# Summary scores on the whole array, and a planner that picks PSUM banks by first release, with measured durations and later landings

## The chip, the cores and the metric

The kernel runs on one core of one Trainium2 chip. The metric is the time on the device in microseconds (us), the median over runs. Lines such as L939 are lines of the kernel before.

The engines have these names in the profile: PE is TensorE (matrix products, written to the eight banks of PSUM), PEld its loading of weights, DVE is VectorE, ACT is ScalarE, POOL is GpSimd, SP is SyncE, which here only issues DMAs. Each engine works through a queue of its own in order; semaphores hold an instruction until its inputs are there.

## The reference, cut to what matters

Attention in which each query sees its neighbours within 16 positions and one summary per block of 32 keys, then eight experts over all tokens, weighted by a routing matrix that is normalised by rows and columns eight times. There are 4 batches, 8 heads, 768 positions and 64 values per head; block is 32 and window 16; N is 3072 tokens of 512 values, E is 8 and F 1024.

```python
    k_sum = k.reshape(B, H, nb, block, D).max(axis=3)
    v_sum = v.reshape(B, H, nb, block, D).mean(axis=3)
    scores_l = scale * np.matmul(q, k.transpose(0, 1, 3, 2))
...
    mask_l = np.abs(pos[:, None] - pos[None, :]) < window
    scores_s = scale * np.einsum('bhsd,bhnd->bhsn', q, k_sum)
    scores_s = scores_s + np.log(block)
    scores_l_m = np.where(mask_l, scores_l, -1000000000.0)
...
    a = a / (np.sum(a, axis=-1, keepdims=True) + 1e-09)
    v_all = np.concatenate([v, v_sum], axis=2)
    return np.matmul(a, v_all).astype(np.float32)
...
    P = np.exp(logits)
    for _ in range(8):
        P /= P.sum(1, keepdims=True) + 1e-09
        P /= P.sum(0, keepdims=True) + 1e-09
        P *= N / E
...
    for e in range(E):
        h = np.maximum(x @ w1[e], 0.0)
        ye = h @ w2[e]
        out += P[:, e:e + 1] * ye
```

## The kernel before

**Stages.** The first part (up to about 169 us) holds the attention, expert 0, the routing and the beginning of expert 1, interleaved. The rest (L1217 on) runs experts 1 to 7 in a fixed order written out by hand, with a scheme that forms a block product from seven instead of eight smaller products; the change does not touch its instructions.

**Attention.** The unit of work is a pair of heads; there are 16 pairs, four for each of the four batches. Pairs 0 to 3 are worked in two halves of 384 queries (`pair_half`, L691), so that expert 0 can begin early; pairs 4 to 15 are worked whole (`pair_whole`, L721). For each pair, POOL issues the loads of k, q and v (`load_pair`, L642); k and q are transposed, on PE and copied out by ACT or DVE (`tr`, L306, and `tr_out`), or for pairs 12 to 15 by a DMA from SP (`tr_dma`, L318). The local scores (`scores`, L379) are matmuls of 64 rows, one head in each half of the array; ACT takes the exponential, DVE multiplies with the band mask (`masks`), and for whole pairs DVE copies the strips that reach into the next block of 128 keys into a shared tile (`edges`). `key_max` (L336) reduces the keys of the pair to 24 maxima for each of the two heads in one DVE instruction, with the head in the upper or lower 64 partitions of `ksT`. The summary scores multiply these with the queries: `summaries` (L427) for a half pair, two matmuls of 64 rows by 32 columns; `summaries2` (L436) for a whole pair, four of them, into two banks. `block_sums` (L351) forms the block sums of v with constant weights `m_blk`, six different ones of 128 columns. `values` and `values_h` bring it together in a bank `av`; DVE normalizes (`normalize`, L510); the result is transposed on PE (`to_xT`) or, for pairs 10 to 14, by a DMA from SP (`x_dma`, L323), and lands in `xT`. `near_values` (L369) is four small DMAs from SP for each whole pair.

**Expert 0 and routing.** As soon as a batch's `xT` is there, `expert0` (L758) computes it in halves of 384 tokens: eight hidden units (L208), relu on ACT or DVE, then six projections of half the depth (L218). `logits` (L537) gives the routing scores of a batch, with `gate` (L794) as its entry in the plan. After the last batch, `bridge` (L1120) adds the eight row and column normalisations, in turn on DVE (sums, reciprocals), POOL (multiplication) and PE (column totals), and the first four groups of expert 1.

**The planner.** All of this is written as units with an engine, a cost in us, dependencies, a priority and the PSUM buffers that they open and use (`Plan.add`). `Plan.order` (L58) simulates the engines when the kernel is built, and emits the units in the order of simulated start times; that becomes each engine's queue. Nothing of it is decided on the chip: if an input comes later than the plan thought, the engine waits and everything behind it in that queue waits too. Four things set the simulated times: the cost of a unit; `HOP`, 0.15 us between engines; `RESHAPE`, 0.1 us when PE goes from one form of the array (`shape`) to another; and `lag`, the time from the end of an issue until a DMA has landed. Gaps of PE of over 0.22 us before the first hidden unit is evacuated are filled with idle matmuls (`keep_busy`, L562, and L852).

**PSUM banks.** The stage has tags m (3 banks), a (3 banks) and s (one buffer of two banks). Within a tag the banks are used in turn: a unit that opens a buffer takes the bank that follows the last one, and waits until that bank's last reader is done. The pools give the tiles out in the same turn (`bank`, L258).

**Loads.** The loads form one chain on POOL (`load`, L637): each is issued after the one before. In the plan a load lands 0.4 us after its share of the DMA engines' time.

## Time and profile before

| | us |
|---|---|
| median of the runs shown (3) | 676.51 |
| their range | 675.13 to 679.61 |
| the profiled execution | 676.52 |
| its span, from the first to the last instruction | 674.8 |
| PE busy in the span | 660.7 |
| DVE busy | 578.9 |
| ACT busy | 404.6 |
| POOL busy | 132.6 |
| mean granted clock of PE | 0.999 |

The profile is a page with several parts and a trace that answers questions. A line of a group reads: line of the kernel, engine, operation, output<-inputs by the program's names, shapes, count, then the busy time in us and the mean of one in ns, then the idle time of the engine just before them and what ended it. A timeline line reads: start, length, engine, line, operation; several that follow each other are merged, with their count. Lists of waits read: who waited, for whom, us in total, how often, the longest. Matmuls are pipelined, so the recorded length of one is longer than the time until the next one starts; the pace is read from start to start.

### The profile page before, as it was taken

Reading aid. Unit: us, or ns where it says so; the run is one execution under the profiler, and the core shown is the slowest. Engines: PE = TensorE matmul, PEld = TensorE weight load, DVE = VectorE, ACT = ScalarE, POOL = GpSimd, SP = SyncE. Lnnn points to the kernel's source line nnn. Section 1 sums busy time; section 2 is a strip of 40 time slices with the busy share of each in tenths; the row PEclk is TensorE's granted clock in tenths of the full one; section 3 lists DMA queues with packets and bytes.
Section 4 is the critical chain, followed back from the end, with each engine's and each line's share of the span. In section 5 each row is a group of like instructions: output and inputs, shape, how many; then the busy total and the mean of one; then the engine's idle time right before and its main releaser. Section 6 shows DMA issues by size and latency. Waiting matters only on the chain.

```text
span 674.8 us, 13527 instructions
## 1 busy us (share of the span) xinstructions
PE 660.7 (98%) x5107; PEld 434.0 (64%) x5107; DVE 578.9 (86%) x1434; ACT 404.6 (60%) x787; POOL 132.6 (20%) x177
## 2 busy tenths in 40 slices
PE   8899998999999999999999999999999999999996
PEld 4566655555666666666666666666666666666665
DVE  7778896776799988998799988998899879998885
ACT  5678885565777765555655565555555565556551
POOL 8599631121101010201010010101020101100001
PEclk9999999999999999999999999999999999999999
DMA  9999999000513050311422051306031232201224
GB/s 119 187 145 146 135 117 154 1 1 1 79 11 37 1 79 1 36 13 23 57 23 27 1 78 11 39 1 79 1 34 16 25 55 23 26 1 53 88 80 157
DMA packets 124018, 36.46 MB, mean 54 GB/s; under 512 B 110384, under 2 KB 121136, under 8 KB 123952
## 3 DMA queue, kind: packets, MB, share of 16 engines
q0 software_dynamic: 104672, 26.22, 43.4%
q1 hardware_dynamic: 18464, 8.83, 6.7%
q8 instruction: 40, 0.66, 0.4%
q10 hardware_dynamic: 816, 0.54, 0.2%
q14 instruction: 26, 0.21, 0.1%
HBM read 52.45 MB, written 6.29 MB: 87 GB/s over the span
## 4 chain that ended last, share of the span: by engine, by line
PE 88%; DMA 5%; DVE 4%; POOL 1%; issue 1%; ACT 0%; DVEq 0%; ACTq 0%
PE xy L939 36%; PE pg L933 16%; PE pb L933 11%; PE pa L933 10%; PE yps L218 5%; PE hps L208 4%; DMA xT<-xs 2%; DMA qst<-in_q_dram 2%; DMA w<-in_moe_w_dram 1%; PE sg L344 1%; PE tkq L315 1%; DVE xs L521 1%; PE vs L354 1%; PE tx L528 0%; DVE hf L883 0%
## 5 line engine op out<-in xcount | busy, mean ns | idle before, releaser
L939 PEld LDWEIGHTS <-hf 128*128 128x128 f16 x2352 | 230.1, 98 | 96.9 <-issue 2.3
L939 PE MATMUL xy<-w,hf 128*128 128x256 f16 x1312 | 183.4, 273 | 0.1
L939 PE MATMUL xy<-ws,hf 128*128 128x256 f16 x984 | 147.6, 273 | 0.4
L199 ACT ACTIVATE hf<-pg 128x512 f16<-128x512 f32 x84 | 50.2, 597 | 150.4 <-PE pg L933 150.4
L1075 DVE SCALAR_TENSOR_TENSOR out_acc<-xy,P_sb,out_acc 128x512 f32<-128x512 f32 x164 | 115.0, 742 | 1.7 <-PE xy L939 1.7
L880 DVE TENSOR_TENSOR hf<-hf 128x512 f16<-128x512 f16 x252 | 99.8, 423 | 8.8
L933 PE MATMUL pa<-xT,w 128*128 128x512 f16 x336 | 99.9, 379 | 0.0
L933 PEld LDWEIGHTS <-w 128*128 128x128 f16 x672 | 65.8, 98 | 43.8 <-issue 0.2
L883 DVE TENSOR_TENSOR hf<-pb,c 128x512 f16<-128x512 f32 x84 | 58.1, 691 | 38.8 <-PE pb L933 35.0
L184 POOL DMA_DIRECT2D w<-in_moe_w_dram x56 | 41.7, 756 | 221.1 <-PE pg L933 192.4
L933 PEld LDWEIGHTS <-ws 128*128 128x128 f16 x504 | 49.3, 98 | 25.3
L967 ACT COPY c<-pg 128x512 f32<-128x512 f32 x84 | 49.3, 586 | 22.4 <-PE pg L933 22.4
L883 DVE TENSOR_TENSOR hf<-pg,c 128x512 f16<-128x512 f32 x84 | 57.1, 679 | 0.7 <-PE pg L933 0.7
L952 ACT COPY pg<-pa 128x512 f32<-128x512 f32 x84 | 47.9, 570 | 4.8
L199 ACT ACTIVATE hf<-pa 128x512 f16<-128x512 f32 x84 | 50.6, 602 | 0.0
L960 ACT COPY c<-pb 128x512 f32<-128x512 f32 x84 | 49.7, 592 | 0.7 <-PE pb L933 0.5
L933 PE MATMUL pg<-xTs,w 128*128 128x512 f16 x168 | 50.0, 379 | 0.1
L933 PE MATMUL pg<-xTs,ws 128*128 128x512 f16 x168 | 50.0, 379 | 0.0
L933 PE MATMUL pb<-xT,ws 128*128 128x512 f16 x168 | 50.0, 379 | 0.0
L933 PE MATMUL pg<-xT,w 128*128 128x512 f16 x168 | 50.0, 379 | 0.0
L933 PE MATMUL pb<-xTs,ws 128*128 128x512 f16 x168 | 50.0, 379 | 0.0
L208 PE MATMUL hps<-xT,w 128*128 128x384 f16 x256 | 48.9, 326 | 0.0
(143 smaller groups left out, 819.6 us busy)
## 6 DMA issues: line engine op xcount, KB each, us to landing
w<-in_moe_w_dram POOLq DMA_DIRECT2D x8, 1024.0 KB, 9.0
w<-in_moe_w_dram POOLq DMA_DIRECT2D x56, 128.0 KB, 3.6
out_dram<-out_acc SPq DMA_DIRECT2D x20, 256.0 KB, 2.0
qst<-in_q_dram POOLq DMA_DIRECT2D x32, 96.0 KB, 6.0
vx<-in_v_dram POOLq DMA_DIRECT2D x16, 192.0 KB, 6.6
kst<-in_k_dram POOLq DMA_DIRECT2D x24, 96.0 KB, 6.2
w<-in_moe_w_dram POOLq DMA_DIRECT2D x2, 512.0 KB, 8.7
kst<-in_k_dram POOLq DMA_DIRECT2D x4, 192.0 KB, 4.9
```

The source lines that it names most:

```text
L184: nc.gpsimd.dma_start(out=t[:, :, h, :], in_=moe_w1[e].rearrange("(dk p) f -> p dk f", p=128)[:, :, f:f + 128])
L199: nc.scalar.activation(out=out, in_=in_, func=AF.Relu, bias=0.0, scale=1.0)
L208: nc.tensor.matmul(hp[:, 0:n], lhsT=w1s[e][:, dk, 128 * f:128 * (f + 1)], rhs=xT[:, dk, t0:t0 + n], start=(dk == 0), stop=(dk == KD - 1))
L218: nc.tensor.matmul(yp[:], lhsT=h[:, f, c * 128:(c + 1) * 128], rhs=w2s[e][:, f, :], start=(f == 0), stop=(f == KF - 1))
L880: nc.vector.tensor_tensor(out=out, in0=in0, in1=in1, op=ALU.subtract)
L883: nc.vector.tensor_tensor(out=out, in0=in0, in1=in1, op=ALU.add)
L933: nc.tensor.matmul(bank[:], lhsT=w[:, dk, :], rhs=x[:, dk, :], start=start and dk == 0, stop=dk == KH - 1, skip_group_check=True)
L939: nc.tensor.matmul(bank, lhsT=a(f)[:, 128 * c:128 * (c + 1)], rhs=w[:, f, :], start=start and f == 0, stop=f == FH - 1, skip_group_check=True)
L952: nc.scalar.copy(out=B["g"][:], in_=B["a"][:])
L960: nc.scalar.copy(out=B["c5"][:], in_=B["b"][:])
L967: nc.scalar.copy(out=B["c2"][:], in_=B["g"][:])
L1075: nc.vector.scalar_tensor_tensor(out=acc, in0=src, scalar=P_sb[:, t, e:e + 1], in1=acc, op0=ALU.mult, op1=ALU.add)
```

## The change

Seven things change, all in the first part.

1. `key_max` writes the maxima to a scratch tile, and a DVE multiply with a constant `own` (ones where the partition belongs to the head, zeros elsewhere) spreads them over a 128-column `ksT`: head 0 in columns 0 to 23 with the lower partitions zero, head 1 in columns 32 to 55 with the upper ones zero, zeros in the rest.
2. The summary scores become one matmul of 128 rows by 128 columns for each half; `summaries2` goes, and whole pairs call `summaries` twice, each with a bank of its own. The exponential reads partitions 0 to 63 in all cases.
3. `m_blk` becomes one strip of 148 columns; the six weights are windows of it that overlap.
4. The planner keeps no turn: a unit takes, of the banks of its tag whose readers are all placed, the one that is released first in the plan. Each bank is a tag of its own in the pool.
5. `HOP` becomes 0.23 us after PE and 0.1 us after any other engine.
6. Costs and lags of units change. The diff shows those that the text speaks of; the costs of the products of expert 0, of `logits` and of the output transposes change by 0.04 us or less, and that of the load of w2 by 0.2.
7. The normalisations' lag for `columns` becomes 0.7 us in place of 2.0 (first) and 1.2.

```diff
-    HOP = 0.15
+    HOP = {"PE": 0.23}
...
     def __init__(self, slots, idle=None):
-        self.slots, self.idle, self.shape = {}, idle, None
-        self.ring, self.turn, self.free, self.waiting = {}, {}, {}, []
+        self.idle, self.shape = idle, None
+        self.ring, self.free, self.waiting, self.now = {}, {}, [], []
...
-            self.slots[t], self.ring[t], self.turn[t] = n, [None] * n, 0
+            self.ring[t] = [None] * n
...
     def order(self):
-        free, ring, turn, waiting = self.free, self.ring, self.turn, self.waiting
+        free, ring, waiting = self.free, self.ring, self.waiting
...
+        def hop(x, e):
+            return 0.0 if x.on == e else self.HOP.get(x.on, 0.1)
+
         def ready(u):
-            t = 0.0
-            for i, b in enumerate(u.opens):
-                old = ring[b.tag][(turn[b.tag] + i) % self.slots[b.tag]]
-                if old is not None:
-                    if any(x.start is None for x in old.users):
-                        return None
-                    t = max([t] + [x.end + (self.HOP if x.on not in u.eng else 0.0) for x in old.users])
+            t, u.slots = 0.0, []
+            for b in u.opens:
+                at = []
+                for n, old in enumerate(ring[b.tag]):
+                    if (b.tag, n) in u.slots or old is not None and any(x.start is None for x in old.users):
+                        continue
+                    at.append((max([0.0] + [x.end + hop(x, "PE") for x in old.users]) if old else 0.0, n))
+                if not at:
+                    return None
+                t0, n = min(at)
+                u.slots.append((b.tag, n))
+                t = max(t, t0)
...
+
+        def take(u):
+            for b, (tag, n) in zip(u.opens, u.slots):
+                ring[tag][n] = b
+            self.now = [n for _, n in u.slots]
...
-                            + [d.end + d.lag + (self.HOP if d.on != e else 0.0) for d in u.deps])
+                            + [d.end + d.lag + hop(d, e) for d in u.deps])
...
-                    ring["m"][turn["m"] % self.slots["m"]] = x.opens[0]
-                    turn["m"] += 1
+                    take(x)
...
+            if u.slots:
+                t0 = max(t, ready(u))
+                t, end = t0, end + t0 - t
...
-            for b in u.opens:
-                ring[b.tag][turn[b.tag] % self.slots[b.tag]] = b
-                turn[b.tag] += 1
...
+            take(u)
...
-        m_blk = attn.tile([128, G, 128], BF16, name="m_blk")
+        m_blk = attn.tile([128, 4 * (G - 1) + 128], BF16, name="m_blk")
...
-        ksT = [attn.tile([128, 32], BF16, name=f"ksT{i}") for i in range(NB)]
+        ksT = [attn.tile([128, 128], BF16, name=f"ksT{i}") for i in range(NB)]
+        own = attn.tile([128, 2, 24], BF16, name="own")
...
         def bank(tag, name, dtype=FP32):
-            pool, n = (mps, 3) if tag == "m" else (aps, NA)
-            return pool.tile([128, 2048 // mybir.dt.size(dtype)], dtype, tag=tag, name=name, bufs=n)
+            n = plan.now.pop(0) if plan.now else 0
+            return (mps if tag == "m" else aps).tile([128, 2048 // mybir.dt.size(dtype)], dtype, tag=f"{tag}{n}",
+                                                     name=name, bufs=1)
...
         def banks2(name, dtype=FP32):
+            plan.now.pop(0)
...
-            nc.vector.tensor_reduce(out=ksT[r][:, 0:24],
-                                    in_=kT[r][:].rearrange("p (n w) -> p n w", w=32),
+            km = attn.tile([128, 1, 24], BF16, tag="km", name="km", bufs=2)
+            nc.vector.tensor_reduce(out=km[:, 0, :], in_=kT[r][:].rearrange("p (n w) -> p n w", w=32),
...
+            nc.vector.tensor_tensor(out=ksT[r][:, 0:64].rearrange("p (j n) -> p j n", j=2)[:, :, 0:24],
+                                    in0=km[:].to_broadcast([128, 2, 24]), in1=own[:], op=ALU.mult)
...
             for g in range(G):
-                nc.tensor.matmul(vs.rearrange("p (j d) -> p j d", j=2), lhsT=m_blk[:, g, :],
+                nc.tensor.matmul(vs.rearrange("p (j d) -> p j d", j=2), lhsT=m_blk[:, 4 * (G - 1 - g):4 * (G - 1 - g) + 128],
...
-            for j in range(2):
-                p0 = 64 * j
-                nc.tensor.matmul(ss[32 * j:32 * j + 32, 0:HS], lhsT=ksT[r][p0:p0 + 64, :],
-                                 rhs=qT[r][p0:p0 + 64, W + h * HS:W + (h + 1) * HS],
-                                 start=True, stop=True)
-
-        def summaries2(i):
-            r = i % NB
-            ss = at["ss", i, 0], at["ss", i, 1] = bank("a", "ss"), bank("a", "ss")
-            for h in range(2):
-                for j in range(2):
-                    p0, o = 64 * j, 64 * h + 32 * j
-                    nc.tensor.matmul(ss[h][o:o + 32, 0:HS], lhsT=ksT[r][p0:p0 + 64, :],
-                                     rhs=qT[r][p0:p0 + 64, W + h * HS:W + (h + 1) * HS],
-                                     start=True, stop=True)
+            nc.tensor.matmul(ss[:, 0:HS], lhsT=ksT[r][:], rhs=qT[r][:, W + h * HS:W + (h + 1) * HS],
+                             start=True, stop=True)
...
         def summary_exp(i, h):
-            o = 64 * h if i >= PB else 0
...
-                                 in_=at.pop(("ss", i, h))[o:o + 64, 0:HS], func=AF.Exp,
+                                 in_=at.pop(("ss", i, h))[0:64, 0:HS], func=AF.Exp,
...
             for t in ksT:
-                nc.vector.memset(t[:, 24:32], 0.0)
+                nc.vector.memset(t, 0.0)
+            nc.vector.memset(own, 0.0)
+            for j in range(2):
+                nc.vector.memset(own[64 * j:64 * j + 64, j, :], 1.0)
...
-            flat = m_blk[:].rearrange("p g n -> p (g n)")
             for pq in range(4):
                 for o in (pq, 32 + pq):
-                    nc.vector.memset(flat[32 * pq:32 * pq + 32, o:o + 132 * (G - 1) + 1:132], 1.0)
+                    o += 4 * (G - 1)
+                    nc.vector.memset(m_blk[32 * pq:32 * pq + 32, o:o + 1], 1.0)
             for t in V_s:
...
-        def load(key, fn, issue, us, deps=()):
+        def load(key, fn, issue, us, deps=(), late=False):
...
-            U[key] = add("LAND", 0, None, [last[1]], lag=0.4)
+            U[key] = add("LAND", 0, None, [last[1]], lag=1.0 if late else 0.4)
...
-                    load(("v", i), lambda: load_v(i), 1.05, 2.05 if i < PB else 1.5,
-                         [U.get(("A", old, 1)), U.get(("near", old))])
+                    load(("v", i), lambda: load_v(i), 1.05, 2.05 if i < PB else 1.6,
+                         [U.get(("A", old, 1)), U.get(("near", old))], i >= PB)
...
-                         1.4 if i < PB else 1.3, [U.get(("tr", old, z))])
+                         1.4 if i < PB else 1.35, [U.get(("tr", old, z))], i >= PB)
...
                     U["tr", i, z] = U["kT", i, z] = add("SP", 1.25, lambda z=z: tr_dma(i, z),
-                                                        [U["kq"[z], i]] + (war_k, war_q)[z], prio, lag=5.0)
+                                                        [U["kq"[z], i]] + (war_k, war_q)[z], prio, lag=5.5)
...
-                U["tr", i, z] = add("PE", 0.4, lambda z=z: tr(i, z, tag),
+                U["tr", i, z] = add("PE", 0.5 if i < PB else 0.335, lambda z=z: tr(i, z, tag),
...
-            U["km", i] = add("DVE", 0.95, lambda: key_max(i), [U["kT", i, 0]] + war_q[2:], prio)
+            U["km", i] = add("DVE", 1.05, lambda: key_max(i), [U["kT", i, 0]] + war_q[2:], prio)
...
-            U["vs", i] = add("PE", 0.36, lambda: block_sums(i),
+            U["vs", i] = add("PE", 0.345, lambda: block_sums(i),
...
-            U["tr", i, 1] = add("PE", 0.25, lambda: tr_qh(i, h),
+            U["tr", i, 1] = add("PE", 0.28, lambda: tr_qh(i, h),
...
-            U["S", i, h] = add("PE", 0.36, lambda: scores_h(i, h),
+            U["S", i, h] = add("PE", 0.225, lambda: scores_h(i, h),
...
-            U["ss", i, h] = add("PE", 0.22, lambda: summaries(i, h, tag),
-                                [U["km", i], U["kT", i, 1], hist("A", n - 2), hold], prio, opens=[buf], shape="tile")
+            U["ss", i, h] = add("PE", 0.17, lambda: summaries(i, h, tag),
+                                [U["km", i], U["kT", i, 1], hist("A", n - 2), hold], prio, opens=[buf])
             U["sx", i, h] = add("ACT", 0.46, lambda: summary_exp(i, h), [U["ss", i, h]], prio, uses=[buf])
...
             U["near", i] = add("SP", 2.5, lambda: near_values(i), [U["v", i], U.get(("A", i - NE, 1))], prio,
-                               lag=1.9)
+                               lag=4.5)
             for h in range(2):
...
-                U["S", i, h] = add("PE", 0.22, lambda h=h: scores(i, h),
+                U["S", i, h] = add("PE", 0.215, lambda h=h: scores(i, h),
...
-            bufs = [Buffer("a"), Buffer("a")]
-            U["ss", i, 0] = U["ss", i, 1] = add("PE", 0.18, lambda: summaries2(i),
-                                                [U["km", i], U["kT", i, 1], U.get(("A", i - NE, 1))], prio,
-                                                opens=bufs, shape="tile")
-            for h in range(2):
-                U["sx", i, h] = add("ACT", 0.46, lambda h=h: summary_exp(i, h), [U["ss", i, h]], prio,
-                                    uses=[bufs[h]])
             for h in range(2):
...
-                U["A", i, h] = add("PE", 0.37, lambda h=h: values(i, h),
+                U["ss", i, h] = add("PE", 0.17, lambda h=h: summaries(i, h, "a"),
+                                    [U["km", i], U["kT", i, 1], U.get(("A", i - NE, 1))], prio, opens=[buf])
+                U["sx", i, h] = add("ACT", 0.46, lambda h=h: summary_exp(i, h), [U["ss", i, h]], prio, uses=[buf])
+            for h in range(2):
+                buf = Buffer("a")
+                U["A", i, h] = add("PE", 0.36, lambda h=h: values(i, h),
...
                 U["xt", i] = U["x", i] = add("SP", 1.25, lambda: x_dma(i), [U["no", i, 0], U["no", i, 1]], prio,
-                                             lag=4.5)
+                                             lag=6.5)
...
-                    step = add(eng, us, fn, [step], -50.0, opens=o, uses=w, lag=(1.2 if n else 2.0) if fn is columns else 0.0)
+                    step = add(eng, us, fn, [step], -50.0, opens=o, uses=w, lag=0.7 if fn is columns else 0.0)
```

More of the change, by code (lines that the diff above doesn't have):

```diff
@@ L795, in gate @@
             buf = Buffer("a")
-            U["lg", b] = add("PE", 0.65, lambda: logits(b), xs, prio, opens=[buf])
+            U["lg", b] = add("PE", 0.61, lambda: logits(b), xs, prio, opens=[buf])
             U["lo", b] = add("ACT", 0.25, lambda: logits_out(b), [U["lg", b]], prio, uses=[buf])
@@ L815 @@
         zero_w1(1)
-        load("w2", lambda: load_w2(0), 0.85, 5.0)
+        load("w2", lambda: load_w2(0), 0.85, 5.2)
         c0 = add("DVE", 3.8, constants, [], -5.0)
```

12 lines of the change are left out of this document (6 added, 6 removed).

## The prediction, made before the result was known

> **What bounds the kernel now.** First the head of the page, then the busy time by stage (columns: start and end, length, then busy microseconds of PE, PEld, DVE, ACT, POOL, clock, DMA, GB/s).
>
> ```profile
> span 674.8 us, 13527 instructions
> PE 660.7 (98%) x5107; PEld 434.0 (64%) x5107; DVE 578.9 (86%) x1434; ACT 404.6 (60%) x787; POOL 132.6 (20%) x177
> ```
>
> ```profile
> 0.00:21.40 21.40, 17.85 (x243) 10.43 (x244) 17.11 (x90) 11.66 (x17) 17.60 (x28) 1.00 1.32 133
> 21.40:34.00 12.60, 10.89 (x161) 6.85 (x157) 9.48 (x30) 8.98 (x17) 6.95 (x9) 1.00 1.67 188
> 34.00:101.30 67.30, 67.12 (x791) 41.77 (x792) 58.72 (x156) 54.28 (x88) 49.38 (x62) 1.00 2.10 136
> 101.30:119.00 17.70, 15.11 (x161) 9.07 (x159) 12.32 (x39) 9.38 (x19) 2.15 (x3) 1.00 1.37 148
> 119.00:168.80 49.80, 49.80 (x289) 26.37 (x287) 36.17 (x93) 28.27 (x55) 10.72 (x16) 1.00 0.00 1
> 168.80:668.00 499.20, 498.55 (x3463) 338.56 (x3462) 442.34 (x1023) 291.52 (x594) 44.41 (x60) 1.00 0.25 36
> ```
>
> TensorE bounds it. The seven experts from 168.8 us on hold 499.2 us with PE busy for 498.6, and no line of the diff issues an instruction there. The diff acts on the first 168.8 us, and there the work of PE is fixed: attention, expert 0, the first four groups of expert 1. Whatever order the planner writes, the stage ends when that work is done, plus the time in which PE stood still. PE stood still for 3.55 us up to 21.4, 1.71 up to 34, 0.18 up to 101.3, 2.59 up to 119 and 0 after. So after 21.4 there are 4.48 us to win. Next, who made PE wait there (us in total, times, longest):
>
> ```profile
> PE lp L542 <- DMA xT<-xs: 1.6, 1, 1.6
> PE tkq L315 <- DMA qst<-in_q_dram: 0.8, 1, 0.8
> PE tx L528 <- DVE xs L521: 0.7, 2, 0.4
> PE tkq L315 <- DMA kst<-in_k_dram: 0.5, 1, 0.5
> PE tx L528 <- ACT Es L452: 0.3, 1, 0.3
> PE av L424 <- DMA Ve<-vx: 0.3, 1, 0.3
> PE tkq L299 <- DVE h L201: 0.2, 1, 0.2
> ```
>
> These seven rows are the 4.4 us. They are of one kind: an instruction stood in PE's queue ahead of work that was ready, because the plan had taken its input to be there already. Up to 34 us the chain that ended last runs through loads, not PE:
>
> ```profile
> 12.94 7.66 DMA w<-in_moe_w_dram
> ...
> 22.50 11.39 DMA qst<-in_q_dram
> ```
>
> The order of POOL's loads is a chain of its own (line 638) that the diff leaves, so the fourth pair's queries land at 33.9 again, and what PE saves ahead of 21.4 I count at nothing.
>
> **The change, part by part.**
>
> *Later landings and measured durations.* The plan takes a DMA to be there after its issue cost and lag: 1.25 + 4.5 = 5.75 us for an x_dma, 2.5 + 1.9 = 4.4 for near_values. Median times from issue to landing:
>
> ```profile
> Ve<-vx SPq DMA_DIRECT2D x48, 10.2 KB, 5.5
> ...
> xT<-xs SPq DMA_TRANSPOSE x5, 6.8
> kT<-kst SPq DMA_TRANSPOSE x4, 8.0
> qT<-qst SPq DMA_TRANSPOSE x4, 8.6
> ```
>
> An x_dma takes 6.8 and the plan will say 7.75. Near_values issues four DMAs in its 2.5 us, the last some 1.9 us after the first, so it lands after 1.9 + 5.5 = 7.4; the plan will say 7.0. The transposes of kT and qT stay short (6.75 against 8.0 and 8.6), but no PE wait on them stands among the rows. Hence the logits (1.6) are placed behind w2 and w1 products of expert 0 that are ready, and that wait goes wholly; so does the wait for Ve (0.3). The loads of pairs 4 to 15 are taken to land 0.6 us later plus 0.05 to 0.1 each. Waits of 0.5 and 0.8 stand at pair 4, and the hidden units of expert 0 that ran just after them can go ahead of them: 1.0 of 1.3 goes. The two waits of tx (0.7) lie in the last pair's chain, where normalize waited for the x_dma two pairs back; with 2.0 us more lag the plan puts them later, and I take 0.4 of 0.7. The new hops (0.23 after PE, 0.1 after others, before 0.15) and unit costs change no instruction, only the order; I price them with the stalls. SP's own order may move; its issue costs do not, and behind a late x_dma only the last pair's near_values queues.
>
> *Banks by first release.* Before, a unit waits for the next bank in turn even if another is free. Two of the rows are such waits, tx on the bank that Es still read (0.3) and tkq on the one that h read (0.2); I take 0.4 of 0.5. The two halves of a whole pair's summaries also no longer need two free banks at once. A bank that is picked by the plan's release can still be late on the chip; that is among the new stalls below.
>
> Each stall also costs the drain of the matmul ahead of it, which the next would have covered. The rows below show it: a product of 384 columns is recorded with (0.82 for four) but follows the last after 0.66 / 4 = 0.165, so about 0.16 us hang on at the end. Six stalls gone: 6 x 0.16 = 1.0. Sum of the gains: 1.6 + 0.3 + 1.0 + 0.4 + 0.4 + 1.0 = 4.7 us.
>
> New stalls: a fixed lag is wrong whenever a DMA scatters.
>
> ```profile
> DMA to landing us min/median/max: 1.9/5.5/9.0
> ```
>
> That is Ve. The bounds are 0 and the 4.5 us that now stand; nearest is the dense stage, 0.18 us in 67. I take two stalls of 0.4 (the Ve wait with its drain): 0.8.
>
> *Summary scores.* A whole pair now runs four tiles of 64 rows and 32 columns at once; afterwards it runs two full matmuls of 384 columns. PE, in order of time (start, length):
>
> ```profile
> 86.59 0.38 PE L344 MATMUL sg<-qT,kT 64*128 64x160 bf16 x6
> 86.90 0.34 PE L442 MATMUL ss<-qT,ksT 64*32 64x384 bf16 x4
> 87.17 0.39 PE L218 MATMUL yps<-w,h 128*128 128x512 f16 x1
> ```
>
> ```profile
> 91.67 0.82 PE L208 MATMUL hps<-xT,w 128*128 128x384 f16 x4
> 92.33 0.35 PE L418 MATMUL av<-vx,em 128*128 128x65 bf16 x6
> 92.51 0.34 PE L424 MATMUL av<-Ve,Ee 128*128 128x130 bf16 x3
> 92.78 0.34 PE L442 MATMUL ss<-qT,ksT 64*32 64x384 bf16 x4
> 93.06 0.82 PE L208 MATMUL hps<-xT,w 128*128 128x384 f16 x4
> ```
>
> The four tiles take 0.27 to 0.28 from start to the next start. Between full-size neighbours there is a second gap ahead: three av of 0.06 began at 92.51, so 0.09 us passed before 92.78. Alone a call costs 0.37; beside the scores, which switch anyway, 0.28. Two full matmuls cost 2 x 0.163 = 0.33 and switch nothing. Of the twelve, eight stand beside scores (+0.05 each) and four alone (-0.04): +0.2 us. A half pair goes from two tiles to one matmul:
>
> ```profile
> 8.72 0.34 PE L432 MATMUL ss<-qT,ksT 64*32 64x384 bf16 x2
> 8.99 0.61 PE L566 MATMUL idle<-zeros 128*128 128x512 bf16 x2
> ```
>
> 0.27 becomes 0.16, so 0.1 each for the four after 21.4: -0.4. Together -0.2 us, bounded by -1 and +2. [...]
>
> *The multiply behind the key maxima*, 16 new DVE instructions of 128x48, and a wait: it needs the reduce, the scores of the summary need it, and masks and evacuations queue behind it.
>
> ```profile
> L482 DVE TENSOR_TENSOR Eh<-erh,band 128x32 bf16<-128x32 bf16 x8 | 1.3, 167 | 0.0
> L354 PEld LDWEIGHTS <-m_blk 128*128 128x128 bf16 x96 | 6.2, 96 | 1.5
> L492 PEld LDWEIGHTS <-Eh 128*128 128x128 bf16 x128 | 4.5, 98 | 0.7 <-issue 0.2
> ```
>
> At the 167 ns of the nearest row that is 2.7 us of DVE, 2.0 of it after 34, where DVE was busy for 58.7 of 67.3: 8.6 us of cover. Counted at nothing; without cover 2.0. The constants change by one smaller, four larger and three new memsets, of the size of this one or less, under the loads of the start: nothing.
>
> ```profile
> 0.95 0.11 DVE L570 MEMSET ident<- 128x64 uint32 x1
> ```
>
>  The overlapping m_blk makes its weights start at steps of 8 bytes. No row has that; L492 loads at steps of 32 bytes as fast (98 ns) as L354 does at 256 (96). I take 0; if a load took twice as long, 72 of them after 34 would add up to 72 x 0.096 = 6.9, an end I give little weight since no offset shows any effect.
>
> *Routing.* The iterations' lag shrinks from 1.2 and 2.0 to 0.7; they run in a stage in which PE has no gap, so this is worth nothing while they end in time:
>
> ```profile
> L1138 DVE TENSOR_REDUCE csum_sb<-P_sb x8: 484/496/503, 122.6 to 164.2; 128x8 f32<-128x192 f32 x8
> L1151 POOL TENSOR_TENSOR P_sb<-P_sb,crec_sb x8: 588/754/866, 127.1 to 167.8; 128x192 f32<-128x192 f32 x8
> L1031 ACT ACTIVATE out_acc<-out_acc,P_sb x4: 711/720/727, 172.5 to 179.2; 128x512 f32<-128x512 f32 x4
> ```
>
> Eight iterations at (164.2 - 122.6) / 7 = 5.9 us end at 168.4; the first use is at 172.5, 4.1 us later.
>
> **The sum.** The profiled execution took 676.52 us (span 674.8 and 1.7 around it); the median of the runs is 676.51, so one stands for the other. 676.5 - 4.7 + 0.8 - 0.2 = 672.4, rounded to 672.5.
>
> **The rivals.** *The stalls only move.* A new order of everything has errors of its own size; for it speaks that kT and qT stay 1.3 to 1.9 us short, against it the 0.18 us of the dense stage. New stalls of 4.5 in place of 0.8 give 676.2; 675 to 678.
>
> *The start gets denser too.*
>
> ```profile
> L566 PE MATMUL idle<-zeros 128*128 128x512 bf16 x22 | 7.6, 464 | 1.0 <-DVE zeros L569 1.0
> ```
>
> Of these 22 ten open the kernel (line 571) and twelve fill gaps, at 0.22 in the plan 2.6 us. If 2.4 to 5 of these and the 3.55 us up to 21.4 turn into earlier hidden units, it ends at 667 to 670. Against it: the load chain to 33.9.
>
> *Routing becomes the end* (slower). Near_values (+2.6) and x_dma (+2.0) push the last pairs in the plan, so the gate could start up to 4.6 to 7 us later, twice for two pairs in sequence. PE would go on, but P is first used 4.1 us after it is ready: from a delay of 4.1 plus the 4 us that PE gains, each microsecond counts. At unchanged pace a delay of 7 gives 676.5 + 7 - 4.1 = 679.4; a delay of 12, 684.4. Against it: those lags only match what the DMAs already take, and 0.6 us less per iteration returns some 4 us.
>
> *The tiles were worth more than the switches, or m_blk's loads slow down.* If a switch saved gives nothing back, twelve whole pairs take 12 x 0.163 = 2.0 us more and half pairs the same: 676.5 - 4.7 + 0.8 + 2.0 = 674.6. With the slow loads, 672.4 + 6.9 = 679.3. Against both: the 0.09 us gap before 92.78, and L492.
>
> **How the numbers follow.** Forecast (670 to 675) 0.54, stalls move 0.20, denser start 0.11, routing 0.10, tiles or loads 0.05. Range 669 to 678: it leaves out the routing case and about half of the denser start, 0.16. One per cent (6.8 us) is about what a measurement of this kernel can tell from no change. Faster by over 1% (under 669.7): 0.10, nearly all of the denser start. Slower (over 683.3): 0.05, half of the routing case. Between: 0.85.
>
> **What would show it.** Right: after 21.4 PE idle of about 1.5 instead of 4.5 us, no wait of lp on xT; the 24 summary matmuls of the whole pairs paced at 0.163 without gaps around them; iterations near 5.3 us. Wrong: waits of PE on kT or qT, on a bank's reader, on the multiply; m_blk loads over 100 ns; a last P_sb later than its first user's turn; the experts' 499.2 us changed.

## The result, and the profile after

The median went from 676.62 us (675.13 to 679.61, five runs) to 672.71 us (672.24 to 673.75, five runs): a ratio of 0.9946, 95% interval 0.9928 to 0.9964, or 3.9 us less. The forecast was 672.5. The profiled execution of the new kernel took 673.7 us, at the upper end of its five; that of before took 676.5, near its median. So the traces have 2.8 of the 3.9 us to explain.

The head of the page of the new kernel, and its busy time by stage (start and end, length, busy time of PE, PEld, DVE, ACT and POOL, clock, DMA, GB/s), the stages cut as in the prediction:

```profile
span 671.9 us, 13501 instructions
```

```profile
0.00:21.40 21.40, 19.10 (x226) 10.68 (x227) 17.64 (x97) 10.85 (x15) 17.44 (x28) 1.00 1.32 132
21.40:34.00 12.60, 12.60 (x186) 8.50 (x185) 9.92 (x28) 9.25 (x17) 7.65 (x10) 1.00 1.66 188
34.00:101.30 67.30, 66.56 (x764) 42.72 (x761) 60.58 (x170) 50.18 (x83) 46.82 (x59) 1.00 1.96 134
101.30:119.00 17.70, 17.14 (x170) 9.76 (x164) 14.03 (x43) 9.62 (x19) 3.88 (x6) 1.00 1.47 155
119.00:168.80 49.80, 48.53 (x287) 26.16 (x288) 36.81 (x98) 28.95 (x56) 11.53 (x19) 1.00 0.01 1
```

The 1.71 us in which PE stood between 21.4 and 34 are gone, and of the 2.59 up to 119 there are 0.56 left. But 0.74 instead of 0.18 stand in the dense stage, and 1.27 in a stage that had none. Most of these are waits that were not there before. All waits of PE from 20 us to the first matmul behind the stage (total, times, longest):

```profile
PE tx L532 <- DVE xs L525: 1.3, 3, 0.7
PE xy L944 <- ACT out_acc L217: 0.7, 1, 0.7
PE av L436 <- ACT kT L217: 0.5, 1, 0.5
PE sg L362 <- ACT er L407: 0.2, 1, 0.2
```

The waits for DMAs (logits on xT, transposes on k and q, values on Ve) have all gone. In their place stand a longer wait of tx and three waits for a bank's reader (xy, av and sg, 1.4 us together), of which xy is the handover to the hand-written part. The tx wait goes back to a store of the last batch. SP issued the store of pair 13 at 107.40, and DVE, which needs the buffer that it reads, waited until 118.62, 11.2 us later:

```profile
107.40 1.23 SPq L340 DMA_TRANSPOSE xT<-xs  x1
```

```profile
118.62 0.56 DVE L525 TENSOR_TENSOR xs<-av,rc 128x384 f16<-128x384 f32 x1 [1.95 <-DMA xT<-xs]
```

Where did the 2.9 us of span go? In both kernels the first xy matmul starts the part after the stage. From it to the end:

```profile
168.77:674.80 506.03, 499.94 (x3473) 339.57 (x3471) 445.06 (x1028) 291.99 (x595) 45.82 (x62) 1.00 0.25 38
```

```profile
167.38:671.90 504.52, 499.30 (x3472) 339.57 (x3471) 445.49 (x1028) 291.23 (x594) 45.50 (x62) 1.00 0.25 39
```

The stage gave 168.77 - 167.38 = 1.4 us, and the part behind it 506.03 - 504.52 = 1.5, though the change does not touch its instructions. I can name no cause for that second half, but two thirds of it look like more than scatter. From the first to the last start of a PE matmul of that part it is 500.3 us in before and 499.3 in after, and handover and w2_late, which have the order of after on PE, DVE, ACT and SP, repeat its 499.3; before_tolerance has 500.1, the other kernels below 498.9 to 500.0. As three executions of one order agree so closely, this 1.0 us is more likely a matter of the order than of chance. The other 0.5 us is the tail behind the last matmul, 5.45 us in before and in old_costs and 4.9 to 5.2 in the rest.

To compare fourteen kernels I use one number: the time in which PE stood between 21.4 us and the first xy, the length of that stretch less PE's busy time. For before and after:

```profile
21.40:168.77 147.37, 142.89 (x1398) 84.02 (x1395) 116.69 (x316) 100.91 (x176) 69.19 (x88) 1.00 1.27 96
```

```profile
21.40:167.38 145.98, 143.42 (x1388) 86.25 (x1386) 121.34 (x336) 97.31 (x171) 68.46 (x89) 1.00 1.23 97
```

It fell from 147.37 - 142.89 = 4.48 to 145.98 - 143.42 = 2.56 us. PE's busy time in the stretch is not quite the same everywhere: 142.5 to 145.3 us, by its idle matmuls, by the work that was already done at 21.4, and in some by the granted clock (0.50 for 3.41 us in both, reshape and tolerance_both). The number therefore tells how much PE stood, and not alone how long the stage took: before_landings stands 0.3 us less than before and reaches xy 1.1 us later.

### The profile page after: what moved, and what is told of

Read it like the earlier page. It is cut to its first block, busy times and chain, and to the rows that moved or that the text cites. A ratio compares the mean times of both kernels' runs of the same rounds, so it can differ in the third digit from the quotient of the medians.

```text
span 671.9 us, 13501 instructions
## 1 busy us (share of the span) xinstructions
PE 661.8 (99%) x5084; PEld 436.5 (65%) x5084; DVE 584.5 (87%) x1460; ACT 399.4 (59%) x780; POOL 131.4 (20%) x177
## 4 chain that ended last, share of the span: by engine, by line
PE 83%; DVE 4%; DMA 2%; issue 1%; ACT 1%; DVEq 0%; ACTq 0%
PE xy L944 37%; PE pg L938 16%; PE pa L938 11%; PE pb L938 11%; PE yps L231 3%; PE hps L221 3%; DMA xT<-xs 2%; DVE xs L525 1%; DVE em L413 1%; DVE km L355 0%; PE py L944 0%; PE tkq L331 0%; PE sg L362 0%; DVE hf L888 0%; DVE h L214 0%
```

## The experiments

All runs beside the kernel before on the same chip (its medians: 676.85 of 33 runs in the first group of four, 676.25 of 23 in the second, 676.30 of 31 in the third). "Stood" is the number just described, "xy" the start of the first xy matmul, both from the one profiled execution of each kernel, whose own time is given too.

| kernel | median (lowest to highest) | ratio, 95% | profiled | xy | stood |
|---|---|---|---|---|---|
| before | 676.62 (675.13 to 679.61) | | 676.5 | 168.77 | 4.48 |
| after | 672.71 (672.24 to 673.75) | 0.9946, 0.9928 to 0.9964 | 673.7 | 167.38 | 2.56 |
| old_landings | 677.37 (674.79 to 681.77) | 1.0013, 0.9995 to 1.0031 | 676.3 | 170.47 | 5.28 |
| banks_in_turn | 677.51 (673.81 to 679.01) | 1.0009, 0.9995 to 1.0024 | 678.1 | 171.21 | 5.26 |
| old_costs | 678.02 (675.70 to 678.98) | 1.0018, 1.0003 to 1.0032 | 677.7 | 171.10 | 5.37 |
| tiles_back | 673.45 (671.70 to 676.43) | 0.9957, 0.9940 to 0.9975 | 673.1 | 167.08 | 2.77 |
| before_landings | 676.33 (675.06 to 677.88) | 1.0002, 0.9992 to 1.0012 | 675.8 | 169.87 | 4.19 |
| before_tolerance | 676.39 (674.86 to 679.33) | 1.0003, 0.9990 to 1.0015 | 675.9 | 168.84 | 4.82 |
| tolerance | 675.03 (672.97 to 677.24) | 0.9977, 0.9964 to 0.9990 | 674.9 | 168.42 | 3.04 |
| reshape | 673.85 (672.69 to 675.97) | 0.9966, 0.9951 to 0.9980 | 676.0 | 170.10 | 4.09 |
| handover | 672.14 (670.95 to 672.73) | 0.9933, 0.9921 to 0.9945 | 671.0 | 164.75 | 0.81 |
| w2_late | 672.13 (671.89 to 672.65) | 0.9935, 0.9922 to 0.9947 | 672.5 | 166.19 | 1.75 |
| both | 673.75 (672.96 to 676.59) | 0.9965, 0.9955 to 0.9975 | 675.9 | 169.41 | 2.76 |
| tolerance_both | 677.63 (675.29 to 679.35) | 1.0018, 1.0005 to 1.0032 | 677.7 | 171.13 | 4.97 |

### One part of the change undone

The theory was that of the prediction: the later landings carry most of the gain, the bank choice a little, costs and tiles nothing. Four kernels each take one part out of the new kernel.

**old_landings**, the lags and load times of before:

```diff
-            U[key] = add("LAND", 0, None, [last[1]], lag=1.0 if late else 0.4)
+            U[key] = add("LAND", 0, None, [last[1]], lag=0.4)
...
-                               lag=4.5)
+                               lag=1.9)
...
-                                             lag=6.5)
+                                             lag=4.5)
```

> The changed kernel with the DMA lags and load times of before (near_values 1.9, x_dma 4.5, transposes 5.0, loads 0.4), all else changed. Theory (the later landings carry most of the gain, 3.6 of the 4.7 us that I summed): about 675.5 to 676.5, ratio to before 0.998 to 1.000, and waits of PE on DMAs after 21.4 us back to 1.5 us or more, among them the logits. Rivals (bank choice, whole-array summaries, or costs and hops carry it): 674 or less, no such waits of over 0.5 us.

**banks_in_turn**, the next bank in turn instead of the one that is released first:

```diff
-                for n, old in enumerate(ring[b.tag]):
...
-                t0, n = min(at)
+                n = (self.turn.get(b.tag, 0) + i) % len(ring[b.tag])
+                old = ring[b.tag][n]
```

> The changed kernel with each tag's banks taken in turn, as before. Theory (bank choice is worth 0.7 us with the drains): 672.5 to 674. Rival (bank choice carries the gain): 675 or more, with waits of PE on readers of banks of 2 us or more after 21.4 us.

**old_costs**, the hop of 0.15 us and the unit costs of before:

```diff
-    HOP = {"PE": 0.23}
+    HOP = 0.15
...
-            U["vs", i] = add("PE", 0.345, lambda: block_sums(i),
+            U["vs", i] = add("PE", 0.36, lambda: block_sums(i),
```

> The changed kernel with the hop of 0.15 us everywhere and the unit costs of before; lags, banks and summaries changed. Theory (costs and hops only reorder; counted at nothing): 672 to 674. Rival (measured durations carry the gain): 675 or more.

**tiles_back**, the summaries, the key maxima and `m_blk` of before under the new planner:

```diff
-            nc.tensor.matmul(ss[:, 0:HS], lhsT=ksT[r][:], rhs=qT[r][:, W + h * HS:W + (h + 1) * HS],
-                             start=True, stop=True)
+            for j in range(2):
+                p0 = 64 * j
+                nc.tensor.matmul(ss[32 * j:32 * j + 32, 0:HS], lhsT=ksT[r][p0:p0 + 64, :],
...
+        def summaries2(i):
...
+            for h in range(2):
+                for j in range(2):
+                    p0, o = 64 * j, 64 * h + 32 * j
+                    nc.tensor.matmul(ss[h][o:o + 32, 0:HS], lhsT=ksT[r][p0:p0 + 64, :],
```

> The changed kernel with the summary scores in tiles of 64 rows by 32 columns, the maxima and the block weights as before, planner all changed. Theory (the tiles cost what the switches cost; 0.2 us apart): 672.2 to 673.6. Rival (whole-array summaries carry the gain): 675 or more. Rival that tiling was worth 2 us: 670.5 to 671.5.

The tiles came out as expected: 673.45, nothing that the intervals could tell from the new kernel. The three planner parts did not: taking out any one of them gives all of the gain back, and PE stands for 5.3 us each time. Gains that add up cannot do this. The stalls are not all the old ones either. The largest waits of PE in old_landings, banks_in_turn and old_costs, the wait of its very first idle matmul left aside:

```profile
PE tx L532 <- DVE xs L525: 1.9, 4, 1.1
PE av L442 <- DMA Ve<-vx: 0.9, 1, 0.9
PE ss L448 <- DVE xs L525: 0.7, 1, 0.7
```

```profile
PE ss L445 <- DVE xs L522: 2.0, 1, 2.0
PE tx L529 <- DVE xs L522: 1.0, 3, 0.4
PE av L439 <- DMA Ve<-vx: 0.9, 1, 0.9
```

```profile
PE av L442 <- DMA Ve<-vx: 2.6, 3, 1.9
PE tkq L331 <- DVE Ve L379: 2.0, 1, 2.0
PE ss L448 <- DVE ksT L357: 0.4, 1, 0.4
```

The wait of the logits, for 1.6 us the largest of before, comes back in none of them, not even with the old landings. What stands is the last pairs' normalise, Ve, and in old_costs a tile of DVE; the section on the new kernel's own waits comes back to the first two.

### One part alone, and orders thrown at random

Two readings were left: the planner needs its parts together, or any change of the order throws dice and the new kernel was a lucky throw. **before_landings** puts the later landings alone into the kernel before (the diff of old_landings the other way round).

> The kernel before with only the later landings and the load times of the new planner; scores on tiles, banks in turn, old costs, one hop of 0.15. Theory that the parts need one another (undoing landings, bank choice or costs alone gave 677.4, 677.5 and 678.0, as much as the kernel before): 675.5 to 677.5, no gain. Rival, the prices of the prediction, which add up (landings alone carry 3.6 of the gain): 673 to 674. Rival, that any change of the order throws dice: anywhere from 672 to 678.

It gained nothing (676.33). Its trace shows where the gain went. The two largest waits of PE:

```profile
PE av L424 <- DMA Ve<-vx: 3.4, 3, 1.4
PE tx L528 <- DVE xs L521: 0.4, 1, 0.4
```

The three waits that the landings were to cure (logits 1.6, q 0.8, k 0.5) are gone, as forecast. A wait of 3.4 us for Ve has come, where there was one of 0.3. SP's queue, in order of time:

```profile
72.87 1.24 SPq L320 DMA_TRANSPOSE kT<-kst  x1
74.28 1.27 SPq L320 DMA_TRANSPOSE qT<-qst  x1
78.86 1.25 SPq L320 DMA_TRANSPOSE kT<-kst  x1
80.22 0.59 SPq L374 DMA_DIRECT2D Ve<-vx  x1
```

and among the waits of SP from 60 to 120 us:

```profile
SPq L320 <- DMA kst<-in_k_dram: 3.4, 2, 3.2
```

A transpose of a late pair stood at the head of SP's queue for 3.2 us until its keys had come, and the near values of an earlier pair, which PE needed sooner, stood behind it: issued from 80.22 on, they had landed at 89.38. PE's row for it:

```profile
89.52 0.40 PE L424 MATMUL av<-Ve,Ee 128*128 128x130 bf16 x3 [1.32 <-DMA Ve<-vx]
```

So 1.3 of the 3.4 us go back to that transpose. The largest of the three, 1.4 us at 112.41, does not: those near values were issued at 102.82 to 104.81 with nothing late ahead of them, and took 7.5 to 8.0 us to land.

Then two kernels that change a number which stands for nothing on the chip, once in the new planner and once in the old. **tolerance** and **before_tolerance**:

```diff
-            t, u, cost = min((x for x in c if x[0] <= t_min + 0.02), key=lambda x: (
+            t, u, cost = min((x for x in c if x[0] <= t_min + 0.01), key=lambda x: (
```

> The new kernel with one number of the planner's choice changed that stands for nothing on the chip: units count as ready together within 0.01 us, not 0.02. Another order, with the same costs, landings and banks. Theory that a faithful plan makes the gain: 671.5 to 674. Rival, that the new order was a lucky throw: back towards 675 to 678.

> The kernel before with the tolerance of 0.01 us and nothing else: another order of the old planner. Theory that the old planner's orders as a class are worse: 675.5 to 678.5. Rival, that the kernel before was an unlucky throw: 671 to 675.

And a third order of the new planner, **reshape**: `RESHAPE = 0.09` for 0.1.

> The new kernel with the planner's price of a change of the array's shape at 0.09 and not 0.10 us, a difference that no unit on the chip has. A third order with the new costs, landings and banks. Theory that the new planner's orders as a class are better: 672 to 675. Rival, luck: 675 to 678.

The three orders of the new planner give 672.71, 673.85 and 675.03, the two of the old 676.62 and 676.39. So both readings hold a part. The new planner's orders are better as a class, as far as five orders can say: their mean, 673.9, is 2.6 us under that of the old ones, and all three lie under both; if the planners were alike, chance would do that in one draw of ten. And the throw is worth up to 2.3 us: the order of the new kernel lies 1.2 us under the mean of its class. The forecast for tolerance, 671.5 to 674, missed by 1.0, and its 675.03 falls where the rival of the lucky throw had it (675 to 678).

### The new kernel's own waits

Two waits of the new kernel could be attacked on their own. The first xy takes the place of the bank that was allocated first, m0, and in the new order the last product of expert 0 lies in m0 too, so that xy waits until ACT has copied it. (In old_landings and banks_in_turn the last product lies in m0 as well, with the same wait; in tiles_back and old_costs it lies in m2 and m1, with none.) **handover** lets the opening idle matmuls take m1 first, with the same order of everything:

```diff
-            n = plan.now.pop(0) if plan.now else 0
+            n = plan.now.pop(0) if plan.now else 1
```

> The new kernel with the same order, but the first bank that is allocated is m1 and not m0, so that the first xy tile, which takes the place of the bank allocated first, does not fall on the bank of the last yps. In the new kernel the first xy matmul waits 0.7 us for the copy of that bank and starts 0.84 us late. Theory that the address makes the wait: no wait of xy on out_acc, and 0.6 to 0.9 us less than the new kernel's 672.7, so 671.8 to 672.1. Rival, that the wait belongs to the last copy wherever it lies: 672.7 and the same wait.

The median is 672.14, at the edge of the forecast (671.8 to 672.1). In the profile xy follows without a wait:

```profile
162.81 2.10 PE L231 MATMUL yps<-w,h 128*128 128x512 f16 x9
164.75 0.60 PE L944 MATMUL xy<-w,hf 128*128 128x256 f16 x4
```

(162.81 + 9 x 0.216 = 164.75.) The theory of the address holds. The intervals of the two ratios overlap, so it is the trace that shows the gain; the times alone would not. The profiled execution, the fastest of the five, also lacks the late store, with no edit made for it: pair 13's store was issued at 107.03 and the normalise behind it ran at 116.34 without waiting.

**w2_late** holds back the 1 MB load of expert 1's w2, issued in the new kernel at 104.22, until pair 14's store has landed, by a copy of one element that reads what the store wrote:

```diff
+            nc.gpsimd.tensor_copy(out=held[0:1, 0:1], in_=xT[0:1, 14 % PB, (14 // PB) * S:(14 // PB) * S + 1])
...
+        last[0] = add("POOL", 0.1, hold_w2, [last[0], U["x", 14]])
         load("w2n", lambda: load_w2(1), 0.85, 5.0)
```

> The new kernel with the load of expert 1's w2 held back on GpSimd until the transposed store of pair 14 has landed. In the new kernel pair 13's store took 11.1 us and landed just after that load, and tx waited 0.88 and 0.52 us behind it. Theory that the load slows the store: it lands in 6 to 7.5 us, the normalise of pair 15 does not wait 1.95 us, and the time is 1.0 to 1.4 less than the new kernel's 672.7: 671.3 to 671.7. Rival, that the store is slow by itself (queue of SyncE): 672.7, and the same two waits. Rival, that the load comes late for expert 1: a wait on w2 near the first yp of expert 1 and 673 or more.

The median is 672.13, and the wait of the normalise is gone (DVE):

```profile
116.71 0.20 DVE L524 RECIPROCAL rc<-av 128x6 f32<-128x6 f32 x1 [1.07 <-PE av L442]
116.94 0.56 DVE L525 TENSOR_TENSOR xs<-av,rc 128x384 f16<-128x384 f32 x1
```

That is the theory's sign, with 0.6 us and not 1.0 to 1.4. Since the store was early enough in handover too, without the edit, these two traces alone would not show that the load slows it. All fourteen do. From issue to landing pair 13's store took 7.9 to 12.1 us in the eleven executions that had the load of w2 in flight beside it (11.1 in after, 9.2 in handover, just in time), 4.3 in w2_late, and 2.8 in the two kernels below that hold back the loads of w1 as well. The five stores in after, w2_late and both:

```profile
DMA to landing us min/median/max: 2.7/5.9/11.1
```

```profile
DMA to landing us min/median/max: 2.8/4.0/6.6
```

```profile
DMA to landing us min/median/max: 2.7/2.7/3.8
```

The near values of the last pair go the same way: 5.5 to 11.0 us in the twelve kernels in which loads of expert 1's weights are in flight beside them, 1.9 to 3.6 in the two that hold them all back. And this is where most orders stall again. Between 98 and 123 us PE waits 1.1 to 2.9 us in ten of the kernels, nearly all of it for the last pairs' stores, through DVE's normalise or the logits, or for their Ve: 2.6 in before, 1.1 in after, 2.9 in banks_in_turn, 2.6 in reshape. In handover and w2_late it does not wait there at all, nor in the two kernels below for either of these.

**both** was to join the two, and **tolerance_both** to see whether the poorer order of tolerance suffers from the same two causes. Here I held back not only w2 but also the four loads of w1, behind the same landing:

```diff
         last[0] = add("POOL", 0.3, hold, [last[0]] + [U["kT", i, 1] for i in range(12, NP)])
+        last[0] = add("POOL", 0.3, hold_x, [last[0], U["x", 14]])
```

> The new kernel, its first bank at the address of m1 and all of expert 1's weights (the four loads of w1 and that of w2) held on GpSimd until pair 14's transposed store has landed. Theory that the waits found in the new kernel are separate and each goes with its cause: no wait of xy, no tx behind a late store, stalls after 21.4 us under 1.5 us where the new kernel has 3.5, and 671.0 to 671.8. Rival, that one of the two repairs takes what the other gave: 672.1, as each alone. Rival, that the held weights come late: a wait on w1 near the first matmul of expert 1 and more than 672.7.

> The kernel with the tolerance of 0.01 us (675.0; its profile shows 1.27 us of av on Ve, 0.84 of xy on the last bank, 0.52 of tx, and two normalises behind stores that took 10 us) with both repairs. Theory that the order is as good as the new kernel's and only meets the same two causes oftener: 671.5 to 673. Rival, that this order is worse by itself, in its waits on Ve or elsewhere: 674 to 675.

Both lost: 673.75 and 677.63, worse than the kernels they were to mend. The wait of xy for the last copy is gone in the two kernels (in tolerance_both xy waits 0.3 us for another reader), but a new wait stands in each profile, in both:

```profile
PE sink L1152 <- DVE csum_sb L1147: 2.0, 1, 2.0
```

and of 3.8 us in tolerance_both. DVE in both shows where it comes from:

```profile
121.86 0.29 DVE L892 TENSOR_TENSOR ws<-w 128x256 f16<-128x256 f16 x1 [3.56 <-DMA w<-in_moe_w_dram]
...
130.07 0.49 DVE L1147 TENSOR_REDUCE csum_sb<-P_sb 128x8 f32<-128x192 f32 x1
```

Before it multiplies with w1, expert 1 has DVE form sums of its parts (ws). These stand in DVE's queue ahead of the routing's column sums, and PE's column total (sink) stands in PE's queue ahead of everything else. The loads that I moved out of the way of one DMA thus held up DVE, and DVE held up PE. The plan could not foresee it, for in it the sums of w1 (`Wt` in `bridge`) depend on no load at all, while those of w2 depend on theirs: it went on placing ws where the weights used to be there long before. My rival had the place wrong: I looked for the late weights at the first matmul of expert 1, and they came out in the routing. Holding back w2 alone together with handover was not tried, so no kernel here joins the two gains of 0.6.

The stall had a price beyond its length. PE stood from 128.5 to 130.6 in both, and then (start and end, length, busy time of PE, PEld, DVE, ACT and POOL, clock, DMA, GB/s):

```profile
128.55:131.96 3.41, 1.46 (x8) 0.66 (x8) 3.38 (x8) 0.35 (x1) 0.00 (x0) 1.00 1.15 183
131.96:135.37 3.41, 3.41 (x9) 1.22 (x8) 3.34 (x10) 0.58 (x1) 1.16 (x2) 0.50 0.12 20
135.37:138.78 3.41, 3.41 (x19) 1.71 (x18) 1.21 (x4) 1.18 (x2) 0.00 (x0) 1.00 0.00 0
```

The granted clock fell to half for 3.4 us. Eight products of 512 columns in that time:

```profile
132.41 3.36 PE L231 MATMUL yps<-w,h 128*128 128x512 f16 x8
135.61 0.59 PE L942 MATMUL pg<-xTs,w 128*128 128x512 f16 x2
```

135.61 - 132.41 = 3.20 us where eight at 0.216 take 1.73: 1.5 us lost on top of the 2.1. The profile of reshape shows the same behind its tx wait of 2.1 us (half the clock from 120.15 to 123.56), and it is the longest of its runs.

In the profiles of before (longest stall 1.74 us) and of after (0.88) the clock stays at 1.00 up to PE's last matmul.

## Why the prediction was right, and where it was not

*The bound, the direction and the total* were right. TensorE bounds the kernel; its standing time fell; none of the four waits on loads and stores that the prediction listed is left; the sum, 672.5, is 0.2 us from the median. That it comes so close is luck in part. The whole forecast gain of 4.0 us lay in the stage, and in the profiled executions the stage gave 1.4. Another 1.5 came from the part behind it, and the rest of the 3.9 is that the profiled execution of the new kernel lies 1.0 above its median.

*The division of the gains failed.* The prediction gave the landings 3.6 us with their drains, the banks 0.7, and costs and hops nothing ("change no instruction, only the order; I price them with the stalls"). Undoing costs alone lost 5.3 us, undoing banks 4.8, undoing landings 4.7, and landings alone gained 0. Each of these is one other order, and orders of one planner lie up to 2.3 us apart; but costs, forecast at nothing, banks, at 0.7, and landings alone, at 3.6, are further off than that. The terms were not separable: a wait that is read off a trace says what was late in that order. It is not a sum of money that one edit pays back, for the edit makes another order, with other waits. The unit to forecast would have been the class: how much does PE stand on average over the orders of a planner?

*"SP's own order may move; its issue costs do not, and behind a late x_dma only the last pair's near_values queues."* As a rule this step failed, though the new kernel has no wait of PE for Ve. In the kernel before_landings near values queued behind a transpose whose keys were late, for 3.2 us, and PE waited 1.3 us for them. There the rival came true that the stalls only move, at a place where the prediction saw no queue.

*New stalls, 0.8 us.* Mis-sized: PE stood for 2.56 us where about 1.5 was forecast, and the four rows of waits of the new kernel sum to 2.7. Three of them, 1.4 us, are waits for a bank's reader, which the prediction had named as a sign of being wrong. One that I did not have among the candidates at all was the handover (0.84 from start to start), which depends on the bank in which the last product of a plan lies. The tx wait behind a late store was to fall from 0.7 to 0.3 and rose to 1.3: two more microseconds of lag make the plan say 7.75 for a store, and beside the load of w2 it took 11.1.

*Summaries, -0.2 us.* Not contradicted: tiles_back, at 673.45 against 672.71, is another order too, and no difference of 0.2 us can be read from two orders. The local price was right. The two matmuls follow without a gap, and what comes next begins 0.34 us later; 0.33 was forecast:

```profile
87.63 0.50 PE L448 MATMUL ss<-qT,ksT 128*128 128x384 bf16 x2
87.97 0.81 PE L221 MATMUL hps<-xT,w 128*128 128x384 f16 x4
```

The four tiles of before thus cost about what the two full matmuls of after do: 0.28 to 0.37 us against 0.34.

*The multiply and `m_blk`, nothing.* Right: no PE wait on the multiply in the new kernel (0.2 to 0.4 us in old_costs, banks_in_turn, tolerance and tolerance_both), and the weights that start at steps of 8 bytes load as fast as before (96 ns):

```profile
L372 PEld LDWEIGHTS <-m_blk x96: 95/96/99, 8.6 to 107.0; 128*128 128x128 bf16 x96
```

*Routing, nothing.* Right: (162.1 - 124.8) / 7 = 5.33 us for an iteration, where 5.3 was forecast, and P is used 5.8 us after it is ready:

```profile
L1143 DVE TENSOR_REDUCE csum_sb<-P_sb x8: 486/492/505, 124.8 to 162.1; 128x8 f32<-128x192 f32 x8
L1156 POOL TENSOR_TENSOR P_sb<-P_sb,crec_sb x8: 588/599/863, 128.7 to 164.7; 128x192 f32<-128x192 f32 x8
L1036 ACT ACTIVATE out_acc<-out_acc,P_sb x24: 715/722/728, 171.1 to 238.8; 128x512 f32<-128x512 f32 x24
```

*Nothing after the stage.* Not confirmed. The prediction named a change of the experts' time as a sign of being wrong, and the profiles differ by 1.5 us there. About 1.0 of it seems to go with the order, as said above; how an order would reach into the part behind it stays open.

So: right in sum because the new planner's orders save about 2.6 us as a class, as far as five orders show, and this one is 1.2 better than its class. The first is what the prediction was after, with the reason open; the second is luck, which no prediction from the profile could have known. Open are what makes the class better (the landings alone and each pair of the three planner parts gave nothing, each in one order), and what changes the time behind the stage.

## What to carry to other kernels

When an order is planned at build time, do not add up the waits of the trace as if each edit cured its own: each edit makes a new order with waits of its own, and here one kind of correction alone, or two of three, gave nothing. Measure the scatter of the planner itself by changing a number that means nothing (here up to 2.3 us between orders) before a gain of that size is put down to an edit. Before a load is moved out of the way, follow what it feeds on every engine's queue, the units that prepare it among them.

## What the runs showed of the hardware

A stall of PE of about 2 us can cost nearly as much again: in both 1.5 us were lost in the eight products behind a stall of 2.1, while the granted clock stood at 0.50. The clock fell to half in four of the profiled executions, each time for 3.41 us: both at 131.96, reshape at 120.15, tolerance_both at 133.42 and before_landings at 18.74. In the 3.41 us just before, PE was busy for 1.46, 1.02, 0.18 and 1.97 us. The last of these had no stall over 1.4 us in it, but several short ones:

```profile
15.33:18.74 3.41, 1.97 (x34) 1.35 (x29) 2.42 (x7) 2.53 (x5) 2.25 (x4) 1.00 1.59 160
18.74:22.15 3.41, 3.41 (x32) 2.11 (x30) 2.39 (x8) 1.15 (x2) 1.99 (x3) 0.50 1.44 194
```

The clock did not fall behind stalls (from start to start, less the pace) of 2.1 and 2.0 us in old_costs, nor behind 2.2 in banks_in_turn (mean granted clock of the two executions 1.0 and 0.999). The 6.83 us around the first of old_costs:

```profile
81.51:84.93 3.42, 2.35 (x24) 1.25 (x22) 0.88 (x1) 3.24 (x6) 0.58 (x2) 1.00 1.98 150
84.93:88.34 3.41, 2.51 (x21) 1.28 (x22) 3.24 (x11) 0.77 (x2) 0.74 (x1) 1.00 2.17 149
```

By the same measure the stalls that it fell behind were 2.1 us in both and 2.3 in reshape (in tolerance_both PE waited for 3.8). So the length of a stall alone does not tell whether the clock falls; what does was not shown. The clock goes with the scatter as well: of the twelve runs of tolerance_both, the one with a mean granted clock of 1.0 took 675.29 us, and two with 0.993 took 679.35 and 678.55.

A transposed store of the same size took 2.8 us from issue to landing with no load of the next weights in flight (both, tolerance_both), 4.3 with the loads of w1 alone (w2_late), and 7.9 to 12.1 beside the load of w2, of 1 MB (pair 13, the other eleven kernels); with the same order on SP and PE it took 9.2 in handover and 11.1 in after. A fixed lag in a plan cannot meet all of these.
